# Value weights cast by a plain copy on Pool, with the gate's factor 0.5 moved into the ScalarE cast of the output weights

## The chip, the core and the metric

The kernel runs on one core of a Trainium2 chip. The metric is device time in microseconds (us) of one execution. Before the change the median of five runs is 195.81 us, and the runs lie between 195.15 and 196.49 us. The core has five engines that matter here: PE (TensorE, matmuls; PEld is its weight load), DVE (VectorE), ACT (ScalarE), POOL (GpSimd) and SP (SyncE, which here only issues DMAs). Each engine takes its instructions strictly in the order in which the program gives them; semaphores tie the engines together.

## The reference

Two layers follow each other. The first is attention over 8 batches of 8 heads, 576 positions and 64 features, with a mask that is causal by blocks of 64. The second takes the result as x and computes a gated linear unit:

```
scores = q @ k^T / sqrt(64), masked by blocks;  x = softmax(scores) @ v     (x: 8 x 576 x 512)
gate_pre[s] = sum over k of conv_w[k] * x[s + k - 4]                        (5 taps, per feature)
gate = 1 / (1 + exp(-gate_pre))
out = (gate * (x @ w_val)) @ w_out                                          (w_val, w_out: 512 x 512)
```

The kernel computes the sigmoid as (1 + tanh(gate_pre / 2)) / 2. ACT gives the tanh, DVE multiplies (tanh + 1) by x @ w_val, and the factor one half that is left over stands in a weight matrix.

## The kernel before

The heads are taken in 32 pairs p; four pairs make a batch. For each pair, q, k and v are loaded as f32 by SP, cast to f16 on POOL (lines 124 to 139, `cast_qk` and `cast_v`), q and k are transposed on PE (`trans_mm`, L144) and evicted by DVE (L168). `s_tile` computes transposed scores in three steps into a PSUM tile S (two buffers), and ACT takes their exponential into `pt` (L210; three buffers). `mask` (L226, L228) zeroes the blocked corners of `pt` on POOL. `av` multiplies `pt` by v into the banks G and `norm` divides on DVE (L255, L256). All matmuls share the helper of line 33, so in the profile they are told apart by their tiles.

For the second layer each batch has two halves: `conv` (PE with the diagonal matrices DG, then ACT's tanh at L287), `vals` (x @ w_val on PE, gated by DVE at L299 into `gv`) and the output tiles (gv @ w_out, evicted by ACT and stored by SP).

The weights are prepared once, in the middle of the first pairs:

- `load_w_val` (L396) and `load_w_out` (L400) load 512 KB halves of the weights as f32.
- `scale_w_val` (L411 to L415) runs on POOL four times, once for each block f of 128 rows: it reads f32, permutes the columns (512 columns as 4 x 4 runs of 32), multiplies by 0.5 and writes f16.
- `cast_w_out` (L417 to L419) runs on ACT twice, each 128 x 1024, and casts f32 to f16 (`w16`).
- `permute_w_out` folds `w16` by PE into PSUM, and ACT copies it out (L409).

The order of the work of pairs 2 to 8 is written out by hand in the string SEQ (L426 to L436); the loop at L573 does the other pairs in a fixed pattern. Each token is one step: `S4.2` is score step 2 of pair 4, `A4`, `N4` and `m4` are `av`, `norm` and `mask` of pair 4, `v5` and `q6` are POOL's casts, `T6` and `E6.0` the transposes and their evictions, `w3` is `scale_w_val(3)`, `k1` is `cast_w_out(1)`, `c` is a conv and `S` alone a `vals` step with a PSUM tile S. The stretch that matters is this, with tokens left out:

```
... q5 w3 w2 w1 ... A3 S4.2 S4.1 v4 ... N3 m4 ... w0 ... L1 c ... S5.2 S5.0 A4 N4 S X4 S5.1 ...
... v5 q6 T6 m5 q7 E6.1 E6.0 c S6.0 S6.1 ... v6 ... S ... t2 q8 v7 k1 k0 S7.1 S7.0 D2.0 A6 X5 N6
S7.2 T8 p1 p0 m7 ... V ... q9 v8 S8.0 X6 S8.1 ... A7 T9 N7 ... S8.2 m8 q10 O ...
```

So POOL does w3, w2, w1, then v4, then m4, then w0, v5, q6. PE's A4 needs m4. Below, the functions around the change stand with their lines.

Of the kernel before, what the change touches and what calls it, by code (L numbers as in the profile page):

```python
# [10 lines left out]
def kernel(  # L11
# [10 lines left out]
    nc = tc.nc  # L22
    fp32 = mybir.dt.float32
    fp16 = mybir.dt.float16
    AF = mybir.ActivationFunctionType
    ALU = mybir.AluOpType
# [5 lines left out]
    def mm(out, lhsT, rhs, start=True, stop=True):  # L32
        nc.tensor.matmul(out=out, lhsT=lhsT, rhs=rhs, start=start, stop=stop,  # L33
                         skip_group_check=True)
# [10 lines left out]
    def const(shape, dt, tag):  # L45
        return cpool.tile(shape, dt, tag=tag, name=tag)
# [6 lines left out]
    w_st = const([128, 4, 512], fp32, "w_st")  # L53
    w_st2 = const([128, 4, 512], fp32, "w_st2")
    w16 = const([128, 4, 512], fp16, "w16")
# [17 lines left out]
    def gbank(i):  # L73
        return G[0:128, i] if i < 2 else GS[i - 2][0:128]
# [41 lines left out]
    def cast_tails(b, eng):  # L116
        t = p2.tile([128, 8, 64], fp16, tag="tl16", name="tl16")
        tl16[b] = t
        eng.tensor_copy(out=t[0:128, 0:8, 0:64], in_=tl_st.pop(b)[0:128, 0:8, 0:64])

    def cast_vtail(b):
        nc.gpsimd.tensor_copy(out=v16t[b % 2][0:128, 0:8, 0:64], in_=vtst[b % 2][0:128])

    def cast_qk(p, first=False):
        t = p3.tile([128, 4, 4, 64], fp16, tag="qk16", name="qk16")
        qk16[p] = t
        s = qk_st.pop(p).rearrange("p i h (n d) -> p (i h) n d", n=4)
        o = t[0:128].rearrange("p n e d -> p e n d")
        if first:
            nc.vector.tensor_copy(out=o[:, 0:2], in_=s[:, 0:2])  # L130
            nc.vector.tensor_copy(out=o[:, 2:4], in_=s[:, 2:4])
        else:
            for e in ((slice(0, 2), slice(2, 4)) if p < 7 else (slice(0, 4),)):
                nc.gpsimd.tensor_copy(out=o[:, e], in_=s[:, e])  # L134

    def cast_v(p):
        b, g = divmod(p, 4)
        s = v_st.pop(p)
        nc.gpsimd.tensor_copy(out=v16s[p % NV][0:128, 0:4, 0:2, 0:64], in_=s)  # L139
# [19 lines left out]
    def trans_mm(p):  # L159
        t = qk16.pop(p)  # L160
        for i in range(2):
            for c in range(4):
                for r in range(2):
                    o = 256 * i + 64 * c
                    transpose(half(r)[:, o:o + 64], t[64 * r:64 * r + 64, c, 2 * i:2 * i + 2, 0:64], r)

    def trans_ev(p, r, cp=None):
        (cp or nc.vector.tensor_copy)(  # L168
            out=QK[p // 4 % 2][0:128, p % 4, 0:2, 256 * r:256 * r + 256].rearrange(
                "p i (s n) -> p i s n", n=4),  # L170
            in_=half(r)[:, 0:512].rearrange("p (i n s) -> p i s n", i=2, n=4))

    def xt_mm(p):
        x = x16.pop(p)
        for i in range(5):
            for r in range(2 if i < 4 else 1):
                transpose(half(r)[:, 512 + 64 * i:576 + 64 * i], x[64 * r:64 * r + 64, i, 0:2, 0:64], r)

    def xt_ev(p, r):
        b, g = divmod(p, 4)  # L180
        n = 5 - r
        nc.vector.tensor_copy(  # L182
            out=xts[b % NX][0:128, g, 4:644].rearrange("p (i r s) -> p i r s", r=2, s=64)[:, 0:n, r],
            in_=half(r)[:, 512:512 + 64 * n].rearrange("p (i s) -> p i s", s=64))
# [7 lines left out]
    def s_tile(p, t, dummies=0):  # L192
        b, g = divmod(p, 4)
        t2 = QK[b % 2]
        s = psS.tile([128, 2, 512], fp32, tag="S", name="S")
        for _ in range(dummies):
            mm(s[0:128, 0], wz[0:128, 0:128], wz[0:128])
        if t == 0:
            work = [(0, 0, 0, 512)]
        elif p == 0:  # L200
            work = [(0, 1, 128, 512), (384, 3, 384, 512)] if t == 1 else (
                [(0, 2, 256, 512)] + [(256 + 64 * j, j, 512, 576) for j in range(4)])
        else:
            work = [(0, 1, 128, 576), (448, 0, 512, 576)] if t == 1 else [
                (0, 2, 256, 576), (320, 3, 384, 576)]
        for (o, j, a, e) in work:
            for h in range(2):
                hp = slice(64 * h, 64 * h + 64)
                mm(s[0:128, h, o:o + e - a], t2[hp, g, 1, 128 * j:128 * j + 128], t2[hp, g, 0, a:e])
        nc.scalar.activation(out=pts[p % NPT][0:128, 0:2, 512 * t:512 * t + 512],  # L210
                             in_=s[0:128, 0:2, 0:512], func=AF.Exp, bias=0.0, scale=0.125)
# [12 lines left out]
    def mask(p):  # L224
        pt = pts[p % NPT]
        nc.gpsimd.memset(  # L226
            pt[64:128, 0:2, 0:1536].rearrange("p h (t s) -> p h t s", t=3)[:, :, :, 0:64], 0.0)
        nc.gpsimd.memset(pt[64:128, 0:2, off[p > 0][3] + 384:off[p > 0][3] + 448], 0.0)  # L228
# [31 lines left out]
    def avs(p):  # L260
        av(p, 0, 0)
        av(p, 1, 1)
# [77 lines left out]
    def warm(n, bank=1):  # L340
        for _ in range(n):
            mm(gbank(bank), wz[0:128, 0:128], wz[0:128])
# [65 lines left out]
                mm(s[32 * j:32 * j + 32, i], idfold[rs, 0, 0:32], w16[rs, j, 0:512])  # L408
        nc.scalar.copy(out=w_out_sb[0:128, x:x + 2], in_=s[0:128])  # L409

    def scale_w_val(f, eng):  # L411
        eng.tensor_scalar(  # L412
            out=w_val_sb[0:128, f].rearrange("p (x j i) -> p x j i", x=4, j=4),
            in0=w_st[0:128, f].rearrange("p (j x i) -> p x j i", j=4, x=4),
            scalar1=0.5, scalar2=None, op0=ALU.mult)  # L415

    def cast_w_out(f):  # L417
        nc.scalar.copy(out=w16[0:128, 2 * f:2 * f + 2, 0:512],
                       in_=w_st2[0:128, 2 * f:2 * f + 2, 0:512])  # L419

# [16 lines left out]
    def load(todo):  # L439
        for x in todo.split():  # L440
            i = int(x[1:])
            if i < {"q": NP, "v": NP, "t": B, "x": B, "a": 2, "b": 2}[x[0]]:
                {"q": load_qk1, "v": load_v1, "t": load_tails, "x": load_vtail,
                 "a": load_w_val, "b": load_w_out}[x[0]](i)
# [21 lines left out]
    def gated(work):  # L466
        for w in work.split():
            if w == "O":
                if len(outs) > 1:
                    out2()  # L470
            elif w[0] == "o":
                out(int(w[1]))
            elif w == "c":
                conv(done["c"])
                done["c"] += 1
            else:
                vals(done["v"], {"V": (0, 1), "W": (2, 3), "S": None}[w])
                done["v"] += 1

    def do(seq):  # L480
        for w in seq.split():
            k, x = w[0], w[1:]
            if k in "OocVW" or w == "S":
                gated(w)
            elif k == "S":
                s_tile(*(int(i) for i in x.split(".")))
            elif k == "l":
                load(x)
            elif k == "m":
                mask(int(x))  # L490
            elif k == "q":
                cast_qk(int(x))
            elif k == "Q":
                cast_qk(int(x), first=True)
            elif k == "v":
                cast_v(int(x))
            elif k == "x":
                cast_vtail(int(x))
            elif k == "t":
                cast_tails(int(x), nc.gpsimd)  # L500
            elif k == "T":
                trans_mm(int(x))
            elif k == "E":
                trans_ev(*(int(i) for i in x.split(".")))
            elif k == "X":
                xt_mm(int(x))
            elif k == "Y":
                xt_ev(*(int(i) for i in x.split(".")))
            elif k == "D":
                b, i = (int(i) for i in x.split("."))  # L510
                tails_mm(b, (2 * i, 2 * i + 1))
            elif k == "F":
                b, i, r = (int(i) for i in x.split("."))
                tails_ev(b, (2 * i, 2 * i + 1), (r,))
            elif k == "A":
                avs(int(x))
            elif k == "N":
                norm(int(x))
            elif k == "L":
                s_last(int(x))  # L520
            elif k == "g":
                conv_diagonals()
            elif k == "w":
                scale_w_val(int(x), nc.gpsimd)
            elif k == "k":
                cast_w_out(int(x))
            elif k == "p":
                permute_w_out(2 * int(x))
            elif k == "d":
                warm(int(x), 0)  # L530


    cast_qk(1, first=True)
# [8 lines left out]
    tails_ev(0, range(4), o=0, half=ghalf)  # L542
    conv_weights()
    do(SEQ)


# [106 lines left out]
```

## Time and profile before

| What | Value |
|---|---|
| Median of five runs | 195.81 us |
| The profiled execution's own time | 195.81 us |
| Its span, first to last instruction | 193.7 us |
| Mean granted clock of TensorE | 0.978 |
| PE busy | 176.3 us, 91% of the span |
| ACT busy | 139.8 us, 72% |
| DVE busy | 121.8 us, 63% |
| POOL busy | 87.0 us, 45% |
| Chain that ended last, by engine | PE 77%, DVE 7%, ACT 6%, issue 4%, POOL 3%, DMA 2% |
| L412, the POOL scale of w_val | 4 instructions, 1488 ns each |
| L418, the ACT cast of w_out | 2 instructions, 1042 ns each |

The span is 2.1 us shorter than the time of the same execution; those 2.1 us lie around it. Busy time is the time that an engine spends in instructions. The chain is followed back from the last instruction: at each step to what released it, or to the instruction before it on its engine. Times in the views are microseconds from the start of the span unless ns is written. In a group's line the form `128x512 f16<-128x512 f32` tells partitions and elements written and read, and the number after x is how many such instructions there were. The clock is the share of full speed that TensorE was granted.

### The profile page before, as it was taken

To read this page: it belongs to the slowest core of one execution; us is meant where nothing else is said; L and a number is where in the kernel's file an instruction comes from. 1 tells how busy PE (TensorE), PEld (TensorE's weight loads), DVE (VectorE), ACT (ScalarE), POOL (GpSimd) and SP (SyncE) were. 2 spreads that over 40 slices of the span, in tenths; PEclk is the share of its full clock that TensorE was granted. 3 is DMA by queue.
4 is the path that set the end of the run, shared out by engine and by line. 5 is a ranking of instruction groups with operands and counts; after the bars stand their busy time and mean duration, and the time that the engine had idled before them with its cause. 6 is when DMAs were issued, how large, how long until landed. Compare 5 with 4: busy or idle time off the path is not lost.

```text
span 193.7 us, 9124 instructions
## 1 busy us (share of the span) xinstructions
PE 176.3 (91%) x3936; PEld 113.0 (58%) x3936; DVE 121.8 (63%) x285; ACT 139.8 (72%) x173; POOL 87.0 (45%) x175
## 2 busy tenths in 40 slices
PE   7597794898998899999999999999999999999982
PEld 2264564565656576666666656666666666656640
DVE  5745770667754868676867677667777776553331
ACT  3567865499796788888788868888798979725421
POOL 7365599536363554455444635264534451300000
PEclk9969997899999999999999999999999999999998
DMA  5999969999769997998589958986787541113355
GB/s 197 228 284 229 308 171 272 273 262 240 186 227 259 262 295 188 264 263 240 160 230 270 263 152 250 252 240 202 225 226 213 133 112 58 58 58 115 111 191 184
DMA packets 70337, 40.43 MB, mean 209 GB/s; under 512 B 48149, under 2 KB 64789, under 8 KB 70298
## 3 DMA queue, kind: packets, MB, share of 16 engines
q1 hardware_dynamic: 69882, 39.48, 75.1%
q8 instruction: 30, 0.49, 1.2%
q10 hardware_dynamic: 416, 0.39, 0.6%
q14 instruction: 9, 0.07, 0.1%
HBM read 30.42 MB, written 9.44 MB: 206 GB/s over the span
## 4 chain that ended last, share of the span: by engine, by line
PE 77%; DVE 7%; ACT 6%; issue 4%; POOL 3%; DMA 2%; DVEq 0%; ACTq 0%; POOLq 0%
PE G L33 47%; PE S L33 23%; PE G L144 7%; ACT pt L210 3%; DVE gv L299 3%; DVE qk L168 2%; DMA qks<-in_q_dram 2%; ACT th L287 1%; DVE x L256 1%; POOL w_val L412 1%; ACT osb L459 1%; POOL DG L392 1%; ACT pt L220 1%; POOL qk L134 1%; DVE qk L130 0%
## 5 line engine op out<-in xcount | busy, mean ns | idle before, releaser
L210 ACT ACTIVATE pt<-S 128x1024 f16<-128x1024 f32 x96 | 94.4, 1023 | 25.5 <-PE S L33 24.5
L168 DVE COPY qk<-G 128x512 f16<-128x512 f16 x63 | 42.4, 685 | 16.6 <-PE G L144 16.6
L226 POOL MEMSET pt<- 64x384 f16 x32 | 13.2, 413 | 72.7 <-ACT pt L210 72.6
L299 DVE SCALAR_TENSOR_TENSOR gv<-th,G 128x288 f16<-128x288 f32 (+1 forms) x43 | 23.4, 558 | 28.5 <-ACT th L287 20.2
L33 PE MATMUL S<-qk 64*128 64x64 f16 (+5 forms) x390 | 35.7, 278 | 3.6 <-ACT pt L210 2.3
L33 PE MATMUL G<-v,pt 128*128 128x65 f16 x896 | 35.5, 197 | 3.3 <-POOL pt L226 2.2
L33 PEld LDWEIGHTS <-pt 128*128 128x128 f16 x960 | 32.9, 100 | 5.8 <-POOL pt L226 2.5
L33 PE MATMUL G<-xt,w_val 128*128 128x288 f16 x232 | 33.4, 287 | 0.9 <-DVE x L256 0.9
L134 POOL CAST qk<-qks 128x1024 f16<-128x1024 f32 (+1 forms) x33 | 30.7, 937 | 3.1 <-PE G L33 1.5
L33 PEld LDWEIGHTS <-w_val 128*128 128x128 f16 x256 | 23.4, 99 | 11.1 <-issue 2.7
L33 PE MATMUL G<-w_out,gv 128*128 128x512 f16 x104 | 26.9, 382 | 0.5 <-DVE gv L299 0.5
L256 DVE TENSOR_TENSOR x<-G,rc 128x640 f16<-128x640 f32 x32 | 26.4, 824 | 1.1
L33 PEld LDWEIGHTS <-qk 64*128 64x128 f16 x390 | 12.9, 95 | 20.1 <-issue 12.7
L33 PEld LDWEIGHTS <-gv 128*128 128x128 f16 x144 | 12.0, 98 | 16.1 <-issue 5.0
L139 POOL CAST v<-vs 128x512 f16<-128x512 f32 x32 | 19.8, 620 | 1.2 <-DMA vs<-in_v_dram 0.9
L182 DVE COPY xt<-G 128x320 f16<-128x320 f16 (+1 forms) x64 | 18.0, 297 | 1.2 <-PE G L144 1.2
L33 PE MATMUL S<-xt,DG 32*32 32x288 f16 x640 | 17.4, 288 | 0.4 <-issue 0.3
L33 PEld LDWEIGHTS <-DG 32*32 32x32 f16 x1280 | 12.8, 88 | 8.2 <-issue 6.4
L33 PE MATMUL G<-xt,DG 32*32 32x288 f16 x640 | 16.8, 288 | 0.0
L255 DVE RECIPROCAL rc<-G 128x10 f32<-128x10 f32 x32 | 6.9, 216 | 14.2 <-PE G L33 14.1
L144 PE MATMUL G<-ident,qk 64*128 64x64 f16 x512 | 15.2, 192 | 0.7 <-DVE qk L130 0.3
L336 ACT COPY osb<-G 128x512 f32<-128x512 f32 x24 | 13.9, 581 | 2.3 <-PE G L33 2.3
(55 smaller groups left out, 151.0 us busy)
## 6 DMA issues: line engine op xcount, KB each, us to landing
out_dram<-osb SPq DMA_DIRECT2D x35, 256.0 KB, 2.8
qks<-in_q_dram SPq DMA_DIRECT2D x32, 256.0 KB, 4.4
vs<-in_v_dram SPq DMA_DIRECT2D x64, 128.0 KB, 4.6
qks<-in_k_dram SPq DMA_DIRECT2D x31, 256.0 KB, 4.3
tlst<-in_q_dram SPq DMA_DIRECT2D x8, 128.0 KB, 4.4
tlst<-in_k_dram SPq DMA_DIRECT2D x8, 128.0 KB, 5.0
vtst<-in_v_dram SPq DMA_DIRECT2D x8, 128.0 KB, 4.3
w_st<-in_moe_w_val_dram SPq DMA_DIRECT2D x2, 512.0 KB, 8.2
```

Of the source, the lines that this page charges most:

```text
L33: nc.tensor.matmul(out=out, lhsT=lhsT, rhs=rhs, start=start, stop=stop, skip_group_check=True)
L134: nc.gpsimd.tensor_copy(out=o[:, e], in_=s[:, e])
L139: nc.gpsimd.tensor_copy(out=v16s[p % NV][0:128, 0:4, 0:2, 0:64], in_=s)
L144: nc.tensor.transpose(out=o, in_=x, identity=ident16[hs, hs])
L168: (cp or nc.vector.tensor_copy)(out=QK[p // 4 % 2][0:128, p % 4, 0:2, 256 * r:256 * r + 256].rearrange("p i (s n) -> p i s n", n=4), in_=h ...
L182: nc.vector.tensor_copy(out=xts[b % NX][0:128, g, 4:644].rearrange("p (i r s) -> p i r s", r=2, s=64)[:, 0:n, r], in_=half(r)[:, 512:512 + ...
L210: nc.scalar.activation(out=pts[p % NPT][0:128, 0:2, 512 * t:512 * t + 512], in_=s[0:128, 0:2, 0:512], func=AF.Exp, bias=0.0, scale=0.125)
L226: nc.gpsimd.memset(pt[64:128, 0:2, 0:1536].rearrange("p h (t s) -> p h t s", t=3)[:, :, :, 0:64], 0.0)
L255: nc.vector.reciprocal(out=rc[0:128], in_=O[:, :, :, 64:65])
L256: nc.vector.tensor_tensor(out=x[0:128].rearrange("p i h d -> p h i d"), in0=O[:, :, :, 0:64], in1=rc[0:128].to_broadcast([128, 2, 5, 64]), ...
L299: nc.vector.scalar_tensor_tensor(out=gv[u][0:128, x:x + nx, bi, hf], in0=th[(b, hf)][0:128, x:x + nx], scalar=1.0, in1=r, op0=ALU.add, op1 ...
L336: nc.scalar.copy(out=o[0:128], in_=r[0:128, 0:512])
```

## The change

The four POOL instructions become plain copies with a cast, with the same operands and the same permuted read. The factor 0.5 goes into the two ACT instructions that cast w_out, which become activations with the function Copy and a scale of 0.5. A new token, `e`, is added to the interpreter of SEQ, and SEQ does not use it.

```diff
-    def scale_w_val(f, eng):
-        eng.tensor_scalar(
+    def cast_w_val(f):
+        nc.gpsimd.tensor_copy(
             out=w_val_sb[0:128, f].rearrange("p (x j i) -> p x j i", x=4, j=4),
-            in0=w_st[0:128, f].rearrange("p (j x i) -> p x j i", j=4, x=4),
-            scalar1=0.5, scalar2=None, op0=ALU.mult)
+            in_=w_st[0:128, f].rearrange("p (j x i) -> p x j i", j=4, x=4))
 
     def cast_w_out(f):
-        nc.scalar.copy(out=w16[0:128, 2 * f:2 * f + 2, 0:512],
-                       in_=w_st2[0:128, 2 * f:2 * f + 2, 0:512])
+        nc.scalar.activation(out=w16[0:128, 2 * f:2 * f + 2, 0:512],
+                             in_=w_st2[0:128, 2 * f:2 * f + 2, 0:512],
+                             func=AF.Copy, bias=0.0, scale=0.5)
...
             elif k == "w":
-                scale_w_val(int(x), nc.gpsimd)
+                cast_w_val(int(x))
...
+            elif k == "e":
+                warm(int(x), 2)
```

Built, both programs have the same instructions in the same order on all five engines. The forms differ at these two places only, and each program has one table load on ACT, at its start.

## The prediction

> **What bounds the kernel now.** I read the page's slices first: PE is busy in nine tenths or more of nearly every slice from 60 us on, so there the order of PE's work sets the pace, and the change touches nothing of it. Before 60 us PE has holes. Which hole belongs to the changed lines is told by the chain of work that ended last, asked for the window 29 to 36 us (start, length, what):
>
> ```profile
> 29.30 1.49 POOL w_val L412
> 30.78 0.57 POOL v L139
> 31.40 0.42 POOL pt L226
> 31.82 0.05 issue
> 31.87 1.83 PE G L33 x30
> 33.70 1.77 PE S L33 x8
> 35.49 0.77 DVE gv L299
> ```
>
> The chain passes through the changed instruction. POOL does w3, w2, w1, then v4 (L139), then the mask m4 (L226); A4 (30 matmuls into G) waits for m4. PE's row before it, in the PE timeline, and the whole of POOL's stretch, in the POOL timeline, show how long (start, length, engine):
>
> ```profile
> 29.30 0.39 PE L33 MATMUL S<-qk 64*128 64x512 f16 x2 [0.40 <-ACT th L287]
> 31.87 0.95 PE L33 MATMUL G<-v,pt 128*128 128x65 f16 x14 [2.18 <-POOL pt L226]
> ...
> 26.38 4.40 POOL L412 TENSOR_SCALAR w_val<-w_st 128x512 f16<-128x512 f32 x3 [0.25 <-DMA w_st<-in_moe_w_val_dram]
> 30.73 0.61 POOL L139 CAST v<-vs 128x512 f16<-128x512 f32 x1
> 31.40 0.41 POOL L226 MEMSET pt<- 64x384 f16 x1
> ```
>
> PE idles 2.18 us, from 29.69 to 31.87, and POOL is never idle from 26.38 on. What follows is slow as well. The busy times by window (PE, PEld, DVE, ACT, POOL, granted clock, DMA share, GB/s):
>
> ```profile
> 29.70:31.87 2.17, 0.00 (x1) 0.01 (x1) 0.00 (x0) 1.93 (x3) 2.11 (x4) 0.96 0.96 298
> 31.87:35.20 3.33, 3.33 (x38) 2.70 (x38) 1.04 (x2) 0.00 (x0) 3.25 (x5) 0.52 1.11 303
> ```
>
> After the hole the clock is 0.52. A4 takes 1.83 us and the eight `vals` matmuls 1.77 us; the chain has the same work at full clock at 44.09 (30 matmuls into G in 1.07 us) and at 47.22 (8 in 1.10 us).
>
> **Part 1: four POOL instructions become casts.** The rows (mean ns of one stands after the busy time):
>
> ```profile
> L139 POOL CAST v<-vs 128x512 f16<-128x512 f32 x32 | 19.8, 620 | 1.2 <-DMA vs<-in_v_dram 0.9
> L412 POOL TENSOR_SCALAR w_val<-w_st 128x512 f16<-128x512 f32 x4 | 5.9, 1488 | 0.3 <-DMA w_st<-in_moe_w_val_dram 0.2
> L134 POOL CAST qk<-qks 128x512 f16<-128x512 f32 x8 | 4.7, 614 | 0.2
> L392 POOL TENSOR_TENSOR DG<-idfold,convT 128x640 f16<-128x640 f16 x1 | 1.3, 1265 | 0.0
> ```
>
> The same size and types as a cast cost 614 to 620 ns, also where the written runs are 64 elements long (L134). No row shows a cast that reads runs of 32 as here, so the bounds are 614 ns from below and, from above, the removed row itself, 1488 ns, where the pattern would set the price; the next slowest POOL row of about this size is L392 with 1265 ns. I take 620 ns: three cast rows with different patterns agree within 1%, so it is the nearest.
>
> The Trainium skill, "GPSIMD Engine Reference", section 4.1, speaks against this: it says that one-input elementwise work on that engine is roughly line-rate. L412 has one input and takes 2.4 times a cast of its size, so by the rule its slowness would come from the permuted read, the copy would inherit it, and the sum would be nothing, 195.8 us. The trace shows no one-input arithmetic without the permuted read; I side with the cast rows.
>
> Now POOL's new clock. Back to back, casts start 0.57 us apart. w3 starts at 26.38 as before (it waits for its data), w2 at 26.95. w1 needs the second half of w_val, issued at 19.0 with 8.6 us to landing: 27.65. v4's second load, issued at 20.1 with 8.4 us to landing, is there at 28.5, so v4 runs from 28.55. m4 begins 0.67 us after v4's start, as before, and ends at 29.65. PE is through with its earlier matmul at 29.69. So A4 starts at 29.7: **2.17 us** earlier. POOL stays off the path as long as a cast takes under about 0.75 us (26.38 + 3 x 0.73 + 1.14 = 29.7); above it, 0.3 us come back for each 0.1 us.
>
> w0 follows from 29.8 to 30.4, before `vals` needs it at 30.8. Without the hole I expect no slow clock: A4 1.07 in place of 1.83 and `vals` 1.10 in place of 1.77, **0.76 + 0.67 = 1.43 us**. In all 3.6 us at the end of `vals`, 31.9 in place of 35.47.
>
> Is the next work ready there? `vals` needs S5.2's tile: ACT does its exponential from 29.68 on, 1.0 us, done at 30.7. S5.1 needs S5.0's, done at 31.63; PE reaches it at 32.1. T6 needs q6: v5 and q6 (0.6 + 1.15 us) follow w0 on POOL, and q6's second load, issued at 27.40 with 3.5 us to landing, is there at 30.9, so the cast ends at 32.2 and PE reaches T6 at 32.3. The second conv waits for DVE's gate (L299), which moves with `vals`. So all 3.6 us arrive at the second conv.
>
> **What is late next: transfers.** From 30 to 45 us the DMA share is about 1.0 and more, so I let no load land earlier than before. q8 (issued 34.23, 6.9 us) lands at 41.2, its cast (1.05 us) ends at 42.25; T8 was at 45.45 and would be wanted at 41.85. It is 0.4 late, but PE idles 0.61 us just after T8 and p1, waiting for ACT's exponential, so that hides it. v7 (issued 38.38, 5.8 us) lands at 44.2; its cast and m7 end at 45.3, A7 would be wanted at 45.55: in time. q9 (issued 40.89, 4.8 us) lands at 45.7; after m7 its cast ends at 46.8, T9 would be wanted at 50.16 - 3.6 = 46.55: **0.3 us late**, with nothing beside it that hides it. From 50 us on the casts come some 5 us ahead of the transposes that need them (q11's cast at 54.18, its transposes at 60.77), so later loads can be late without PE noticing.
>
> **Part 2: two ACT instructions change form.** Removed are two CASTs, 128x1024, of 1042 ns (L418). The nearest row of the added form is L210, an activation with a scale of the same size: 1023 ns. So 2 x -0.02 us, with ends of -0.04 and, if the SBUF read costs as now, 0. A table load (L347, 1283 ns) would be the dear case, but the changed program holds only the one at its start, as before. Hidden is little here: ACT is busy for 4.60 of the 5 us from 40 to 45, so 0.1 us more for each would arrive as 0.2 us. I count 0. Their input, w_out, lands at 36.1 and 38.25, and they would start at 38.1 and 39.1. No instruction is moved past another, and no DMA or wait is added.
>
> **Sum.** 2.17 + 1.43 - 0.3 = 3.3 us. The profiled execution took 195.81 us (span 193.7 and 2.1 around it), which is also the median of the runs shown, so the sum stands against both: 195.8 - 3.3 = **192.5 us**, 1.7% less. Its own range is 191.8 to 193.2: the late loads count nothing to 1.0 us, and either side 0.3 us for the scatter of landings.
>
> **Rivals.**
>
> *The pattern sets the price* (the copy also takes 1265 to 1488 ns). For it: L412 and L392 are the only POOL rows of this size with finely cut operands, and both are slow. Against it: L134's cuts cost nothing. At 1265 A4 starts at 26.38 + 3 x 1.245 + 1.14 = 31.25, 0.6 us earlier, and the idle time of 1.55 us may still bring the slow clock: 195.2 us. At 1488: 195.8.
>
> *The slow clock stays, or loads take more.* The clock fell at 31.7 and stayed low for 3.4 us, and a second stretch at 0.50 stands from 11.2 to 14.6 us, as long; what sets their place can't be read here. If the work before 29.7 alone (PE busy 1.30 of 1.70 us) let it fall, only 2.17 - 0.3 would remain: 193.9. Loads that land 1 us later than before would give 193.5. Together 193.2 to 194.8.
>
> *Slower: the permuted copy costs more than the scaled one.* If POOL's copy deals with runs of 32 worse than L412 did, its three instructions ahead of m4 lengthen the hole by 3 x (d - 1.49). It decides against the change from 1.49 us on, and passes what can be told from no change (0.5%, about 1 us, is what a measurement of this kernel can tell) at 1.82. With d = 2.08, two casts of 1041 ns: 3 x 0.59 = 1.8, so 197.6 us. No cast row points there.
>
> *More than the sum*: loads move up with POOL's progress and the chain shortens elsewhere: under 191.8.
>
> **Chances.** The forecast 0.66; clock or loads 0.16; the pattern sets the price 0.11; slower 0.04; more than the sum 0.03. Faster by over 0.5%: 0.66 + 0.16 + 0.03 = 0.85; within 0.5%: 0.11; slower: 0.04. The range goes from 191.8 up to 195.2, the copy at 1265 ns; left out are about 1 in 10 for a copy at the removed row's price or above, and the 0.03.
>
> **What would show it.** In the profile after: the L412 group as CAST with about 620 ns; m4 at about 29.2; no wait of PE for L226 near 30 us; a granted clock of 1.00 from 30 to 35 us; the first `vals` at 30.8; the second conv at 32.7 in place of 36.30; T9 waiting for POOL near 46.7; L417 at 1.02 to 1.04 us. I am wrong if L412 stays above 1 us, if the clock is 0.5 after 30 us all the same, or if the gain at 32 us is given back at loads before 60 us.

## The result and the profile after

The changed kernel takes 194.61 us (median of 27 runs, 191.74 to 199.15) against 196.0 us for the kernel before (48 runs, 193.02 to 199.87). The ratio is 0.9929 with a 95% interval of 0.9901 to 0.9958, so it is faster by 0.7%, about 1.4 us. The forecast was 1.7%. The ratios here leave disturbed executions out; where a mean is given, it is over all executions. Over the executions of this study whose granted clock is on record, 141 of the kernel before have a mean of 196.08 us (standard error 0.10) and 60 of the changed kernel one of 194.83 us (0.22): a gain of 1.26 us, standard error 0.24.

The profiled execution of the changed kernel took 192.39 us with a span of 190.3 us, 3.4 us less than before's 193.7. That is near the forecast's sum, and it is one of the fastest executions; the typical one is 2 us longer. So the one profile answers what the edit does to its stage, and the other executions what becomes of that.

The casts, from the groups kept apart by form (busy us and mean ns of one stand after the bar):

```profile
L412 POOL CAST w_val<-w_st 128x512 f16<-128x512 f32 x4 | 2.4, 619 | 0.1
L417 ACT ACTIVATE w<-w_st 128x1024 f16<-128x1024 f32 x2 | 2.0, 1048 | 0.0
```

POOL's stretch, in the POOL timeline (start, length, engine):

```profile
25.96 1.74 POOL L412 CAST w_val<-w_st 128x512 f16<-128x512 f32 x3
27.63 0.62 POOL L139 CAST v<-vs 128x512 f16<-128x512 f32 x1
28.32 0.41 POOL L226 MEMSET pt<- 64x384 f16 x1
...
28.93 0.61 POOL L412 CAST w_val<-w_st 128x512 f16<-128x512 f32 x1
```

The three casts take 1.74 us where the three scaled ones took 4.40, and the mask is written at 28.32 in place of 31.40. PE, in its timeline:

```profile
29.19 0.39 PE L33 MATMUL S<-qk 64*128 64x512 f16 x2 [0.40 <-ACT th L287]
29.73 0.58 PE L33 MATMUL G<-v,pt 128*128 128x65 f16 x14
...
30.65 1.14 PE L33 MATMUL S<-xt,w_val 128*128 128x288 f16 x8
...
35.06 0.25 PE L33 MATMUL G<-v,pt 128*128 128x65 f16 x3
35.52 0.49 PE L33 MATMUL G<-v,pt 128*128 128x65 f16 x11 [0.21 <-issue]
```

A4 starts at 29.73 with no wait before it, and `vals` at 30.65. The last line is the first sign of what comes: A5 breaks off after its third matmul for 0.21 us, and no engine, only "issue", is named. The same two windows as before (PE, PEld, DVE, ACT, POOL, granted clock, DMA share, GB/s):

```profile
29.70:31.87 2.17, 2.06 (x38) 1.59 (x37) 0.92 (x2) 1.81 (x2) 1.52 (x3) 1.00 0.99 282
31.87:35.20 3.33, 2.59 (x118) 1.78 (x119) 2.27 (x5) 2.40 (x4) 1.36 (x3) 1.00 1.02 323
```

In the first, PE is busy for 2.06 us where it had been busy for nothing; in the second it does 118 matmuls at full clock where it did 38 at 0.52. From the tanh of the first conv to that of the second, in the ACT timelines, 5.33 us remain (28.49 to 33.82) of 8.77 (28.60 to 37.37): 3.4 us of gain at that point.

### The profile page after: what moved, and what is told of

It reads as the page before. It is cut to its first block, busy times and chain, and to the rows that moved or that the text cites. A ratio compares the mean times of both kernels' runs of the same rounds, so it can differ in the third digit from the quotient of the medians.

```text
span 190.3 us, 9124 instructions
## 1 busy us (share of the span) xinstructions
PE 174.0 (91%) x3936; PEld 110.9 (58%) x3936; DVE 121.6 (64%) x285; ACT 139.8 (73%) x173; POOL 83.6 (44%) x175
## 4 chain that ended last, share of the span: by engine, by line
PE 73%; DVE 6%; SPq 4%; ACT 4%; issue 4%; POOL 3%; DMA 3%; POOLq 0%; ACTq 0%; DVEq 0%
PE G L33 46%; PE S L33 21%; PE G L144 7%; DMA vs<-in_v_dram 3%; DVE gv L299 2%; ACT pt L210 2%; SPq L90 2%; DVE qk L168 2%; DVE x L256 1%; POOL qk L134 1%; SPq L110 1%; ACT th L287 1%; SPq L99 1%; ACT osb L459 1%; POOL DG L392 1%
## 5 line engine op out<-in xcount | busy, mean ns | idle before, releaser
L33 PE MATMUL G<-v,pt 128*128 128x65 f16 x896 | 33.9, 194 | 0.8 <-issue 0.2
L134 POOL CAST qk<-qks 128x1024 f16<-128x1024 f32 (+1 forms) x33 | 30.8, 937 | 7.5 <-DMA qks<-in_k_dram 4.0
L33 PEld LDWEIGHTS <-pt 128*128 128x128 f16 x960 | 31.5, 98 | 3.1 <-issue 1.0
L33 PEld LDWEIGHTS <-qk 64*128 64x128 f16 x390 | 12.8, 94 | 20.7 <-issue 12.9
L144 PEld LDWEIGHTS <-qk 64*128 64x128 f16 x512 | 10.8, 95 | 7.1 <-POOL qk L134 1.7
```

The lines of the kernel that those rows point to most:

```text
L144: nc.tensor.transpose(out=o, in_=x, identity=ident16[hs, hs])
```

## The experiments

The expectations below name their theories by letters. Theory L (loads): the gain at 30 us is real in every execution, and loads that come no earlier take part of it back. Theory K (clock): the clock's part of the gain (1.43 us) was one execution's chance, and is not there in others or is lost again elsewhere. Theory H (hole): PE's wait for the mask near 30 us is mostly shorter than the profile's 2.18 us. Theory F (fetch) came up after the first four runs: PE's own instructions come late at fixed counts. The edits are shown against the changed kernel or the kernel before, as their names say. A helper of the dummy kernels is this:

```
def small(n, w, c):
    for _ in range(n):
        mm(gbank(1)[0:w, 0:c], wz[0:128, 0:w], wz[0:128, 0:c])
```

### Both kernels again, unchanged (e1, e2, e12, e16)

> The kernel before, unchanged, to learn the granted clock of its single executions beside their times, and to have a second trace of it. The changed kernel's executions ranged in mean clock from 0.971 to 1.000 and in span from 189.6 to 197.0 us. Theory L (loads): the changed kernel moved up against loads that mostly land later than in the one profiled execution; then before's clocks average well below the changed kernel's (0.978 against about 0.988), the 1.4 us of clock are gained, and what is missing is idle time of PE waiting for casts. Theory K (clock): the stretch at half clock near 31.7 us is not in every execution of before, or returns elsewhere in the changed one; then before's mean clock lies within 0.004 of the changed kernel's. Theory H (hole): PE's wait for L226 near 30 us is mostly shorter than 2.18 us; then a second trace shows under 1.5 us. Time against before: 1.00, by all.

> The changed kernel, unchanged, beside the run of before on the same chip, with a second trace. Ratio 0.993 again by all. Theory L: where its execution is over 193 us, the trace shows POOL waiting for DMA in front of L134 and L139 between 35 and 60 us and PE idle for POOL's casts. Theory K: such an execution shows one or two stretches of 3.4 us at clock 0.50 before 60 us, without more waiting for DMA.

> The changed kernel once more, unchanged, beside these, for the spread of its executions and a third trace: ratio 0.990 to 0.994 by all theories.

> The changed kernel beside them, with a fourth trace. Ratio 0.990 to 0.996. Theory F: if its trace has a pause at number 1217, then the fetch ahead of it started 3 us or more after the block's start, and where it started within 2.3 us there is no pause.

The kernel before gave 195.97 us, ratio 1.0038 (0.9997 to 1.0078). The changed one gave 193.36, 195.07 and 194.42 us, ratios 0.9907 (0.9872 to 0.9943), 0.9957 (0.9920 to 0.9995) and 0.9928 (0.9887 to 0.9969). The stage from tanh to tanh took 8.77 and 7.65 us in two traces of before, and 5.33, 5.33, 6.07 and 5.76 us in four of the changed kernel. So the stage's gain is not the same in each execution, but it is there in each that was traced. Two of the four of the changed kernel are longer for a reason that the traces name: e12 has a pause of 0.41 us in the stage, and in e16 A4 still waits 0.56 us for m4, because v4's load landed 0.86 us after POOL was free for it.

What follows the stage differs. PE's timeline of the repeat e12:

```profile
34.21 0.70 PE L33 MATMUL S<-qk 64*128 64x512 f16 x6 [0.41 <-DVE qk L168]
35.06 0.25 PE L33 MATMUL G<-v,pt 128*128 128x65 f16 x3
36.79 0.76 PE L33 MATMUL G<-v,pt 128*128 128x65 f16 x11 [1.47 <-issue]
```

and the windows of that pause and of what comes after it:

```profile
35.30:36.80 1.50, 0.03 (x2) 0.01 (x1) 0.00 (x0) 1.50 (x2) 0.14 (x1) 1.00 1.15 227
36.80:40.20 3.40, 3.40 (x51) 2.60 (x51) 1.63 (x4) 0.73 (x2) 0.00 (x0) 0.50 1.05 205
```

At the very place of the profiled 0.21 us, PE stands still for 1.47 us, with its clock at 1.00 and no engine late; then it works for 3.4 us at half clock, which costs 1.7 us more. In e2 the same place shows no pause, and there are ones of 0.68 us at 54.58 and 1.04 us at 66.85. In e16 there is no such pause before 88 us. Instead, PE waits for casts of late loads. PE's and POOL's timelines of e16:

```profile
40.88 0.23 PE L144 MATMUL G<-ident,tl 64*128 64x64 f16 x4 [0.98 <-POOL tl L119]
...
43.35 0.41 PE L144 MATMUL G<-ident,qk 64*128 64x64 f16 x16 [0.75 <-POOL qk L134]
```

```profile
40.21 0.62 POOL L119 CAST tl<-tlst 128x512 f16<-128x512 f32 x1 [0.96 <-DMA tlst<-in_k_dram]
```

The cast t2 itself waits 0.96 us for its load, and PE waits for t2, then for q8. So there are two kinds of loss after the stage: pauses without a releaser, and late loads.

### Where the pauses stand

The releaser "issue" means that PE waited for nothing that the profile shows. Counted by position, these pauses are regular. With PE's instructions numbered from 0 in order of start (7878 in the program), every such pause above 0.15 us, 40 in 20 traces, stands ahead of an instruction whose number is 193 above a multiple of 256. A line of the changed kernel's page, the same in before's, fits this (queue, kind: packets, MB, share):

```profile
q8 instruction: 30, 0.49, 1.2%
```

Here q8 is a DMA queue, not the token q8 of SEQ. That is 30 packets for 7878 instructions, one for about 260. I read the queue as PE's instruction fetch; no view names the engine that it serves, but the times fit. Taken in order, one packet belongs to each block of 256 instructions. Ahead of the 40 pauses the packet took 0.9 to 1.6 us and was sent 0.9 to 5.9 us after PE entered the block before, and PE went on 1.2 to 1.9 us after the packet's end. No block in the 20 traces starts less than 1.1 us after its packet's end. The block that matters runs from instruction 961 to 1217: `vals`, the second conv, the S6 steps and the first three matmuls of A5. From the traces:

| Trace | Block's length without the pause, us | Packet sent after the block's start, us | Pause at 1217, us |
|---|---|---|---|
| before | 5.46 | 2.95 | 0.26 |
| e1, before again | 5.41 | 4.71 | 1.86 |
| after | 4.73 | 2.49 | 0.21 |
| e2, changed again | 4.57 | 0.86 | 0 |
| e12, changed again | 4.72 | 3.88 | 1.47 |
| e16, changed again | 4.57 | 1.67 | 0 |

The change takes out what made the block long (half clock, and the wait for w0), so PE comes to its end some 0.8 us sooner, and a packet that is sent more than about 2.3 us after the block's start is late. The kernel before is hit too, but only when the packet is sent later still.

### One part alone: ACT's scale without POOL's cast (e8)

```diff
-            scalar1=0.5, scalar2=None, op0=ALU.mult)
+            scalar1=1.0, scalar2=None, op0=ALU.mult)
...
-        nc.scalar.copy(out=w16[0:128, 2 * f:2 * f + 2, 0:512],
-                       in_=w_st2[0:128, 2 * f:2 * f + 2, 0:512])
+        nc.scalar.activation(out=w16[0:128, 2 * f:2 * f + 2, 0:512],
+                             in_=w_st2[0:128, 2 * f:2 * f + 2, 0:512],
+                             func=AF.Copy, bias=0.0, scale=0.5)
```

> One part alone: the factor 0.5 in ACT's cast of w_out, while POOL's instruction stays a scaled copy with a factor of 1. All theories: ratio 1.00 (0.997 to 1.003), L412 at 1.49 us, the two activations at 1.02 to 1.04 us each.

It took 195.44 us, ratio 0.9990 (0.9950 to 1.0030). The hole ahead of A4 stays (1.90 us). L412 takes 1493 ns with the factor 1, and the two activations 1048 ns. So ACT's part costs and brings nothing that this interval can tell, and the gain at the stage is POOL's.

### The clock by itself: PE kept busy in the hole (e5, before)

Eight full dummies fill the hole, and the eight dummies at the start became 128 small ones, so that 256 instructions more, one block, stand ahead of A4 and the blocks end at the same work.

```diff
-    warm(8)
+    small(128, 32, 32)
...
-        "F1.1.0 Y3.1 d3 L1 Y3.0 c E5.1 E5.0 S5.2 S5.0 A4 N4 S X4 S5.1 lq8 lv8 lv7 lq9 v5 q6 T6 m5 "
+        "F1.1.0 Y3.1 d3 L1 Y3.0 c E5.1 E5.0 S5.2 S5.0 d8 A4 N4 S X4 S5.1 lq8 lv8 lv7 lq9 v5 q6 T6 m5 "
```

> The kernel before with eight dummy matmuls (1.7 us) in PE's hole ahead of A4; the eight large dummies at the very start are replaced by 128 small ones, so that the count of PE instructions ahead of everything else moves by exactly 256 from A4 on. The hole of POOL stays, the clock should not fall after it. Theory K (clock): the share of the lost time that is clock is what this run gains, 0.5 to 1.4 us, ratio 0.993 to 0.998, and no stretch at 0.50 near 31.7 us. Theory F (instruction fetch; found in the traces of the first four runs, where all eleven long pauses of PE that nothing else explains stand at PE's instruction number 193 modulo 256): the gain is given back in part at the next such place, number 1217, in the midst of A5; ratio 0.996 to 1.002.

It took 196.88 us, ratio 1.0026 (0.9989 to 1.0064). PE's timeline:

```profile
30.58 1.89 PE L33 MATMUL G<-wz 128*128 128x512 f16 x8
32.33 0.60 PE L33 MATMUL G<-v,pt 128*128 128x65 f16 x14
...
34.05 1.15 PE L33 MATMUL S<-xt,w_val 128*128 128x288 f16 x8 [0.63 <-POOL w_val L416]
```

and the window after the hole:

```profile
31.70:35.10 3.40, 2.77 (x42) 1.82 (x40) 1.05 (x2) 0.66 (x1) 3.26 (x7) 1.00 1.07 291
```

The clock is 1.00 where it had been 0.52, and in the end nothing is won. At the stage about 1.0 us is: 7.77 us from tanh to tanh, against 8.77 in the profile of before. It is not more because `vals` now waits 0.63 us for w0, which POOL does at the end of its row of scales (L416 is L412 in this kernel). Where that 1.0 us goes later is not shown; no pause stands at the block's end that the expectation named. The repeat e1 shows the same without dummies: a hole of 1.78 us, full clock after it, and a wait of 0.63 us for w0. So 0.63 of the 1.43 us lay over another wait on POOL. The change frees both, so this doesn't shrink the gain at the stage; it shows that the 1.43 us which the forecast put down to the clock were not the clock's alone.

### Fewer loads (e3 and e4, e9 and e10, e13 and e14)

Three cuts, each made to both kernels. In e3 and e4 the first halves of w_val and w_out are not loaded:

```diff
-        "... lq5 la1 E2.1 la0 lv4 A0 "
+        "... lq5 la1 E2.1 lv4 A0 "
...
-        "... m4 lv6 lb1 X3 F1.1.1 lb0 lt2 w0 "
+        "... m4 lv6 lb1 X3 F1.1.1 lt2 w0 "
```

In e9 and e10 q, k and v are not loaded from pair 8 on:

```diff
+        if p >= 8:
+            qk_st[p] = kept[("q", p % 4)]
+            return
...
+        if p >= 8:
+            v_st[p] = kept[("v", p % 4)]
+            return
```

In e13 and e14 w_out is not loaded at all, and ACT's casts read w_val's tile:

```diff
-        "... m4 lv6 lb1 X3 F1.1.1 lb0 lt2 w0 "
+        "... m4 lv6 X3 F1.1.1 lt2 w0 "
```

> The kernel before with half of the weight loads left out: w_val's and w_out's first halves are not loaded, and the four and two casts read the second halves twice, so the output is not the reference's. 1 MB of DMA less between 18 and 38 us; instructions of PE, ACT, DVE and POOL unchanged. Alone it should change before little by Theory K and H (0.995 to 1.00), since POOL's casts, not loads, hold PE up there. By Theory L too: 0.99 to 1.00. It is the base for the next run.

> The changed kernel with the same half of the weight loads left out (output not the reference's). Against the kernel before with the same cut: Theory L expects the full 3.3 us or more, a ratio between the two of 0.983 or less, because loads after 25 us land some 2 us earlier. Theory K expects the gap of the uncut pair, about 1.4 us (0.993), with the clocks of its executions still at 0.97 to 0.99. Theory H the same 1.4 us, with clocks near 0.99.

> The kernel before without the loads of q, k and v from pair 8 on; their casts read what pairs 4 to 7 left in the buffers, so the output is not the reference's. Every instruction of PE, ACT, DVE and POOL stays, and w_val and w_out are loaded as before; from about 33 us on little traffic is left beside the tails and the stores. Base for the next run. Theory F (PE's fetches of 16 KB wait among the loads): no pause of PE over 0.3 us at 193 modulo 256 after 35 us, and executions closer together; median 193.5 to 195.5 us. Theory K alone (clock by the place of windows): 195 to 196.5, spread as before.

> The changed kernel with the same loads left out. Theory F: pauses gone here too, so the gap to the run before this one is what was worked out for the stage, 2.8 to 3.6 us, a ratio between the two of 0.982 to 0.986, and mean clocks of 0.99 to 1.00. Theory K: the gap stays 1.2 to 1.8 us. Theory L: 3.3 us too, but then POOL's waits for DMA in the uncut changed kernel must be seen to hold PE up by over 1 us, and its traces show 0.3 at most.

> The changed kernel without w_out's loads: the ACT casts read w_val's staging tile instead, so the output is not the reference's; 1 MB less traffic between 30 and 38 us, when PE's instruction block for number 1217 is fetched. Theory F: block 961 to 1217 has 4.7 us of work, and the fetch of the next one takes 2.5 to 2.8 us from its start to its use; with less traffic it starts earlier than the 2.5 to 4.0 us after the block's start seen so far, so PE's pause at 1217 is under 0.7 us, mean clock 0.993 or more, and the gap to the kernel before with the same cut is 2.3 to 3.3 us (0.983 to 0.988). If the start of the fetch does not depend on the loads: pause of 1 to 2 us and a gap of 1.2 to 2 us, as now.

> The kernel before with the same cut (output not the reference's), the base of the run before this one. Theory F: its block from 961 to 1217 has 5.4 to 6.5 us of work, the fetch is hidden, and the cut changes little: 0.993 to 1.00.

Measured, with the ratio to the kernel before (unedited) and the difference of the pair's means over all executions:

| Cut | In before: median us, ratio | In the changed kernel: median us, ratio | Difference of means, us |
|---|---|---|---|
| none | 196.0 | 194.61, 0.9929 (0.9901 to 0.9958) | 1.26 ± 0.24 |
| half of w_val and w_out | 195.24, 0.9982 (0.9944 to 1.0019) | 193.63, 0.9899 (0.9859 to 0.9939) | 1.46 ± 0.43 |
| q, k, v from pair 8 on | 193.96, 0.9919 (0.9885 to 0.9952) | 194.50, 0.9852 (0.9774 to 0.9930) | 0.24 ± 0.61 |
| w_out | 195.69, 0.9987 (0.9945 to 1.0029) | 192.22, 0.9816 (0.9765 to 0.9866) | 3.56 ± 0.47 |

The ± are standard errors; with six executions and wide scatter the third row's medians and ratios do not order its pair. Two expectations failed here: Theory L's 3.3 us in the second row, and Theory F's 2.8 to 3.6 us in the third. The last row is the clear one: without w_out's 1 MB the kernel before is not faster, the changed one is, and the pair's difference agrees with the forecast's 3.3 us. PE's timeline in e13:

```profile
34.74 0.58 PE L33 MATMUL G<-v,pt 128*128 128x65 f16 x14
35.16 0.19 PE L33 MATMUL G<-v16t,pt 128*128 128x65 f16 x1
```

A5 runs through, and PE waits for no late cast between 28 and 60 us. In the stretch 33 to 35 us the windows of e13, of the profiled changed kernel and of e12 are, in this order:

```profile
33.00:35.00 2.00, 1.44 (x63) 0.84 (x43) 1.03 (x3) 1.84 (x4) 1.48 (x3) 1.00 0.67 172
```

```profile
33.00:35.00 2.00, 1.51 (x86) 0.84 (x54) 1.35 (x3) 1.84 (x4) 1.16 (x3) 1.00 1.03 332
```

```profile
33.00:35.00 2.00, 1.50 (x86) 0.84 (x54) 1.35 (x3) 1.84 (x4) 1.16 (x3) 1.00 1.00 342
```

The DMA share is 0.67 without w_out and 1.0 with it, and what is loaded behind w_out lands sooner: q8's second load at 37.02 us in e13, at 40.61 in the profiled changed kernel, at 42.10 in e16. Half of the cut was not enough (e4 shows a pause of 2.02 us at instruction 1217 and a half clock after it), and cutting the loads that follow left the pause in place: e10 shows 1.74 us there, with q8's load gone altogether.

### Other instructions at the blocks' ends (e6, e15, e7) and the early half clock (e11)

If the pause goes with the number of the instruction, then instructions put ahead move it to other work. e6 and e15 are the same kernel:

```diff
-    warm(8)
+    small(82, 32, 48)
```

e7 puts 16 instructions ahead:

```diff
-    warm(8)
+    small(16, 128, 256)
```

e11 fills the place where a half clock of 3.4 us stands at about 11 us in the profile of before and in some traces of both kernels' variants:

```diff
-        "E2.0 S1.1 S2.0 S2.1 N0 q3 lv5 v2 m1 q4 S2.2 m2 T3 X0 E3.0 E3.1 d2 A1 Y0.1 Y0.0 lq6 S3.0 "
+        "E2.0 S1.1 e2 S2.0 e2 S2.1 N0 q3 lv5 v2 m1 q4 S2.2 m2 T3 X0 E3.0 E3.1 d2 A1 Y0.1 Y0.0 lq6 S3.0 "
...
+    warm(4, 2)
```

> The changed kernel with the eight large dummy matmuls at the very start replaced by 82 small ones of about the same total time: 148 more PE instructions ahead of all work, nothing else. Theory F: the pauses stay at instruction numbers of 193 modulo 256 and so fall on other work; by the lengths of the blocks of 256 instructions in the changed kernel's traces the blocks that are shorter than 5.2 us miss it by 4.4 us in sum at this shift against 5.6 unshifted, so 0.3 to 1.5 us faster than the changed kernel, ratio 0.984 to 0.991. Theories L and K: as the changed kernel, 0.991 to 0.993, and pauses, if any, in A5 and the same matmuls as before.

> The changed kernel with 148 more PE instructions ahead of all work, a second time, since six executions were too few. Its first trace had no pause before 79 us. Theory F: mean clock above the changed kernel's 0.989 and a median 0.3 to 1 us below it in the same call; if alignment does not matter for the total: the same as the changed kernel within 0.4 us.

> The changed kernel with the eight large dummies at the start cut in sixteen of half the size: 16 more PE instructions, the same time. Theory F: a bad place by the same sum (8.5 us against 5.6), so 1 to 3 us slower than the changed kernel, ratio 0.997 to 1.008, with pauses at 193 modulo 256. Theories L and K: as the changed kernel, 0.991 to 0.993.

> The changed kernel with eight dummy matmuls more, placed where PE waits: four behind the first tails' transposes (a hole of about 1 us at 9 us in every trace) and two each ahead of S2.0 and S2.1 (0.7 and 0.5 us at 15 us), to keep the clock from falling near 11 us, which it did in five of the ten traces. Theory K: the early stretch at 0.50 goes, mean clock 0.995 or more, 0.5 to 1.2 us faster than the changed kernel: ratio 0.983 to 0.989. Theory F alone: no change for it, 0.990 to 0.993.

e6 took 195.08 us, ratio 0.9896 (0.9830 to 0.9963), and its repeat e15 195.07, ratio 0.9950 (0.9905 to 0.9995). e7 took 194.08, ratio 0.9869 (0.9818 to 0.9921), and was expected to be slower. e11 took 194.82, ratio 0.9922 (0.9888 to 0.9956). None can be told from the changed kernel. PE's timeline of e7:

```profile
34.13 0.39 PE L33 MATMUL S<-qk 64*128 64x512 f16 x1 [0.41 <-DVE qk L168]
35.36 0.59 PE L33 MATMUL S<-qk 64*128 64x512 f16 x5 [0.84 <-issue]
```

With 16 instructions ahead the pause stands 16 instructions earlier in the work, after the first S6 matmul and not within A5; the number is 1217 again. In e15 the block's end falls within `vals`, with the longest pause seen:

```profile
42.28 0.40 PE L33 MATMUL S<-xt,w_val 128*128 128x288 f16 x1 [3.39 <-issue]
```

So the place belongs to the instruction count and not to any tile, which is shown. Moving it brought no gain that these runs can tell. e11 held the clock at 1.00 from 11 to 14.6 us in its trace, and had no time to show for it; PE waited 1.12 us for t2 at 40.5 instead. That fits the first profile, in which the changed kernel was 1.0 us ahead at 24 us (no half clock at 11 us there) and then waited 0.91 us for the cast of q5: POOL had been held by the load of t1 (1.18 us ahead of 21.8 us) and came to q5 only 0.1 us sooner than in before.

### Loads in another order (e17, e18)

```diff
-        "... m4 lv6 lb1 X3 F1.1.1 lb0 lt2 w0 "
-        "... A4 N4 S X4 S5.1 lq8 lv8 lv7 lq9 v5 q6 T6 m5 "
-        "q8 v7 k1 k0 S7.1 S7.0 ..."
+        "... m4 lv6 lt2 X3 F1.1.1 lq8 lb1 lb0 w0 "
+        "... A4 N4 S X4 S5.1 lv7 lv8 lq9 v5 q6 T6 m5 "
+        "q8 v7 k1 S7.1 k0 S7.0 ..."
```

Here t2 and q8 are loaded ahead of w_out, and nothing is left out. e18 adds e11's dummies to it.

> The changed kernel with nothing left out, but the tails and q8 loaded ahead of w_out's halves, v7 ahead of v8, and k1 and k0 put behind each other's exponentials (k1 S7.1 k0 S7.0). w_out lands some 2.5 us later, at about 38.5 and 41. If the traffic of w_out ahead of t2, q8 and v7 holds PE up in most executions (1.7 us in the fourth trace of the changed kernel), 0.5 to 1.5 us faster than the changed kernel, 0.984 to 0.990. If the fetch at 1217 is what counts, it only moves along: as the changed kernel, 0.990 to 0.994. Slower, 0.995 or more, if ACT now waits for w_out.

> The same with the eight dummy matmuls of the early stretch as well, which in their first run gave a clock of 0.993 on the mean and no gain in time. By the clock theory 0.3 to 1 us faster than the run before this one; by the first run's result the same as it.

e17 took 194.33 us, ratio 0.9860 (0.9779 to 0.9940), over six executions, and can't be told from the changed kernel. Its own trace (span 189.2 us) has neither a pause nor a wait for a late cast; ACT waits 0.6 us for w_out. e18 took 196.38 us, ratio 1.0000 (0.9955 to 1.0045), though its dummies alone cost nothing in e11. Its trace shows two waits of PE for ACT of 1.2 us at 42 and 44 us and a half clock from 43.5 to 50.3. ACT's timeline tells why it was late there:

```profile
40.20 1.06 ACT L417 ACTIVATE w<-w_st 128x1024 f16<-128x1024 f32 x1 [2.77 <-DMA w_st<-in_moe_w_out_dram]
```

ACT waits 2.77 us for w_out, which the new order loads later, and the exponentials that PE needs stand behind that cast. In e17's trace the same wait was 0.6 us. So no version was found that is surely faster than the changed kernel.

## Why the prediction was right and wrong

- **The cast at 620 ns: right.** It takes 619 ns. The rule of the Trainium skill that spoke against it ("GPSIMD Engine Reference", section 4.1, one-input work at roughly line rate) does not hold for the removed form here: with the same permuted read, the scaled form took 1488 ns and the cast 619, so the pattern alone costs nothing and the scaled form made the difference. No run has the scaled form without the permuted read. The rivals with a dear pattern fell with it.
- **A4 at 29.7, `vals` at 30.8, the second conv at 32.7, clock 1.00: right in the profiled execution** (29.73, 30.65, 32.75, 1.00). m4 came even earlier, as v4's load landed sooner. In e16 it landed later, and A4 waited 0.56 us for m4 after all.
- **Part 2 at nothing: right.** The activation takes 1048 ns where 1023 were expected and 1042 stood before, and e8 moved nothing that can be told.
- **3.6 us at the second conv: too much as a typical value.** It was read from one execution of before. Tanh to tanh, three traces with before's timing (before, e1, e8) took 8.77, 7.65 and 8.97 us, a mean of 8.46, and four of the changed kernel a mean of 5.62: 2.8 us. Three more traces with before's casts, which leave loads out (e3, e9, e14), took 8.96, 9.30 and 8.43 us; with them it is 3.1 us. Nor was the term "0.76 + 0.67 = 1.43 us" the clock's alone (e5).
- **"What is late next: transfers" with 0.3 us: this is the step that failed.** It took the landings of one execution as fixed and asked only for casts. T9 did not wait in the profile after, where q9's second load landed at 44.2 us and not at 45.7. Two other things were late, in some executions and not in others: t2 and q8 (0.98 and 0.75 us in e16), of which the text had not named the first and had called the second hidden, and PE's own instructions at the end of a block (1.47 us in e12), which it did not know of. Such a pause can be followed by a half clock, which is 1.7 us more. Of the 2.8 to 3.1 us won at the stage, 1.26 are left at the end, so 1.5 to 1.8 us are given back after it, an estimate from few traces; the prediction had 0.3. That w_out's loads are behind it is shown by e13 and e14: without them the difference is 3.56 us (standard error 0.47). The prediction's own sign of being wrong, a gain given back before 60 us, is what came, with pauses behind 60 us as well (66.85 us in e2).
- **The clock differs from execution to execution in both kernels.** One stretch at half clock of 3.4 us lowers the mean clock by 0.009. By that measure 3% of before's executions have no such stretch, 60% one, and 37% two or more; of the changed kernel's, 30%, 45% and 25%. The mean clock rises from 0.9866 to 0.9892, worth 0.5 us (0.0026 x 193) at most, not 1.43.
- **Of the rivals, "the slow clock stays, or loads take more" came nearest**, with its time (193.2 to 194.8). Its loads part is near to what happened (in e16 q8's second load landed at 42.10 us, 0.9 us later than in before), but it did not have PE's own instructions; its clock part happened elsewhere than it said, after pauses near 37 us (e12) and not at A4.

**Still open:** how the 1.5 to 1.8 us divide between late casts and late instructions. Without w_out e13's trace shows neither between 28 and 60 us. e10 kept the pause without q8's load, which speaks for the instructions; but packets were also sent early in traces with the loads in place (0.86 us in e2), and e17's interval is too wide. The pair e9 and e10 is not explained either: with the later loads left out the kernel before gains 2.0 us and the changed one 0.9, so that their difference shrinks to 0.24 us (standard error 0.61). Why a packet is sent 0.9 us after a block's start in one execution and 4.7 us in another is not known.

## What to carry to other kernels

Taking a wait out of an early stage is worth its length only as far as what feeds the next stage can come earlier too; where the DMA engines are full, count the landings after the stage as the likely new bound, and include the engine's own instruction stream among them. Take a stage's length, its clock and its landings from several executions before summing them: here the stage took 7.65 to 8.97 us in three traces with the same timing, and the profiled pair lay 3.4 us apart where the means lie 1.3 apart. To test where a lost gain went, make the same cut in both kernels and compare the pairs, as with w_out, whose absence helped only one of the two.

## What the runs showed of the hardware

- A pause of PE without a releaser stands at fixed counts of its instructions, 256 apart, and moves with instructions put ahead (e7: 16). It was up to 3.39 us long (e15), and in some executions of a kernel there is none at a count where another has one (1217: 1.47 us in e12, 0 in e2). PE goes on 1.2 to 1.9 us after a 16 KB packet of queue q8 ends.
- Half-clock stretches are 3.4 us long here (twice that in e18), as the Trainium skill has it for its window ("TensorE: Matmul & The Clock Gate", Part 1). It has them come after at least one idle window of about that length; here a pause of 1.5 us (e12) was enough, and one of 1.78 us (e1, ahead of A4) was not.
- Within a trace the stretches start whole multiples of 3.41 us apart (11.20, 31.68 and 192.11 us in before). Cut into windows on that grid, from 6 us on and without the last 4 us, the 20 traces show PE busy for 17 to 55% of the window ahead of a stretch and for 58% or more of every other window but one (48%, from 30.5 us in e1); the second half of e18's stretch is an exception too. So where a pause falls on the grid counts, and the grid's place differs from one execution to the next.
- The changed kernel scatters by 4% from one execution to the next (191.7 to 199.2 us), with the same program on the same data; its DMA share is about 1.0 or more between 29 and 41 us in the profile.
